# K read by quarters of 512 rows of 16 items and turned contiguously, softmax over two batch rows, five V buffers, and wo behind V: a decode layer on one core

## The chip, the core and the metric

The kernel runs on one core of one Trainium2 chip. What counts is the device time of one execution in microseconds (us). The core's engines work side by side and each takes its own instructions in order: TensorE (PE) multiplies matrices, VectorE (DVE), ScalarE (ACT) and GpSimd (POOL) work on vectors, and SyncE (SP) issues transfers (DMA) on one queue. An instruction or a transfer can wait for others by semaphores, and then all that stands behind it on its engine or queue waits too.

## What is computed

One token for each of 8 batch rows goes through attention and an MLP, each behind a layer norm. There are 32 query heads of width 128 and 8 K/V heads, so 4 query heads share one. Of 8192 cached rows the last 2048 count. The reference, cut:

```
B, D, F = 8, 512, 1792
Hq, Hkv, Sk, Dh, W = 32, 8, 8192, 128, 2048
q = layernorm(x) @ wq                            # wq is 512 x 4096
scores = einsum("bhqd,bhkd->bhqk", q, k_cache[:, :, Sk - W:]) * Dh ** -0.5
p = softmax(scores)
o = einsum("bhqk,bhkd->bhqd", p, v_cache[:, :, Sk - W:])
h = x + o @ wo                                   # wo is 4096 x 512
u = layernorm(h)
out = h + u + gelu(layernorm(u) @ w3) @ w4       # w3 is 512 x 1792, w4 is 1792 x 512
```

The branch of w1 and w2 shifts tokens, and with one token it is zero. All data are bf16. The K and V rows that count are 33.5 MB each, wq and wo 4.2 MB each, w3 and w4 1.8 MB each. An item below is one batch row with one K/V head: 64 items of 2048 rows.

## The kernel before

The work on K goes in 16 tiles of 2 MB. Tile n is batch row n // 2 and 4 of its 8 heads, with all 2048 rows, in two buffers (`knat`). `load` (L627) puts 64 consecutive rows, 16 KB, on each partition; the partition is 4 times the row block (32 of them) plus the head.

`turn_K` (L327) turns a tile on VectorE by transposes of 32x32 blocks of f32, each f32 being two bf16, into `kT_sb`, in four instructions of 128x1024. Its write pattern is scattered: the four heads, which lie side by side in a block, go to places 2 KB apart, so that each head's 512 columns stand in one run for PE:

```
src = knat[:, n % NK, :].bitcast(dt.float32).rearrange("p (c h x) -> p h c x", h=2, x=32)
dst = kT_sb[:, n % NK, :].bitcast(dt.float32).rearrange("p (h t n) -> p h t n", h=2, t=KQ)
parts = [(src[:, h, lo:hi], dst[:, h, :, 8 * lo:8 * hi].rearrange("p t (c a) -> p c a t", a=8))]
```

For the last batch row the pieces are 128x512, eight to a tile.

`pe_QK` (L341) multiplies a tile with a block-diagonal arrangement of q (`qblk`, copied by `keep_q`, L299, half on ScalarE and half on VectorE) into a bank of PSUM for the batch row (`S_ps`). After two tiles a batch row has its scores as 128x512, and the softmax runs: `row_max`, `head_max` (L356 to L368, VectorE), `row_exp` (L370, ScalarE), `turn_P` (L390, a VectorE transpose of 128x512 bf16), `move_P` (L402, 16 small matmuls), `spread_P` (L415, four ScalarE copies into `pT_sb`), and for the sums `row_sums` and `head_sums` (L377 to L387).

V comes in tiles of the same form in three buffers (`vnat`). `pe_PV` (L438) multiplies one with the spread P in 16 matmuls of 512 columns into `o_rows`; `o_parts` (L450) splits the result into two bf16 parts, one copied by ScalarE (L451), the other subtracted by VectorE (L452); `pe_oT` (L455) selects the right columns with matmuls (L461), and `scale` (L468) divides by the sums into `oT_all`. The last V tile comes in four loads of 512 KB with runs of 1 KB and goes another way (`turn_last`, `pe_PVi`).

The order on each engine is written out in `plan` (L528 to L564): each step gets a slot, and the steps are issued by rising slot. For tile n the four transposes have n, n + 0.1, n + 0.2 and n + 0.3, `pe_QK` n + 0.48, `pe_PV` of tile n - 2 comes at n + 0.55, its `o_parts` at n + 1.07 and `pe_oT` at n + 1.22. So on VectorE the subtraction for PV n - 2 stands between the first and the second transpose of tile n + 1, and on PE PV n - 2 stands behind QK n.

The transfers are one list on SP's queue (L642 to L658): wq, K0, K1, then K and V in turns, the first half of wo, the last whole V, the second half of wo, four quarters of the last V, w3 and w4. K n waits for the transposes of tile n - 2, V n for PV n - 3; wo goes into the place of wq (`wbig`), in runs of 1 KB.

The end: `pe_wo_row` (L494) multiplies 16 heads with wo into rows, split and added by `pe_h0` (L509); `pe_wo` (L518) adds the other heads; then come the layer norm (L575 on), `pe_w3` (L590), gelu, w4 (L660 on) and the store.

Of the kernel before, what the change touches and what calls it, by code (L numbers as in the profile page):

```python
# [6 lines left out]
dt = mybir.dt  # L7
ACT = mybir.ActivationFunctionType
ALU = mybir.AluOpType
# [19 lines left out]
NV = 3  # L29
NQ = B * G // KQ  # L30
CQ = W // 32
NR = 4
FQ = CQ * DH

# [31 lines left out]
def bass_sequential_preLN__sliding_block_cached__mixer_s_mlp__decode_kernel(  # L66
# [23 lines left out]
    with es:  # L90
# [8 lines left out]
        sel_f = sb([128, H], dt.float32, "sel_f")  # L99
# [4 lines left out]
        wo_v = wbig[:, :].rearrange("p (h n) -> p h n", h=H)  # L104
        knat = sb([128, NK, FQ], dt.bfloat16, "knat")
        vnat = sb([128, NV, FQ], dt.bfloat16, "vnat")


        kT_sb = sb([128, NK, FQ], dt.bfloat16, "kT_sb")

        w3_sb = knat[:, 1, 0:KC * F].rearrange("p (k f) -> p k f", k=KC)
        w4_sb = kT_sb[:, 0, 0:FC * D].rearrange("p (k n) -> p k n", k=FC)
# [20 lines left out]
        qblk = sb([128, 2, 4 * KQ * B, H], dt.bfloat16, "qblk")  # L133

        P_sb = sb([128, 2, 512], dt.bfloat16, "P_sb")
        pB_sb = sb([128, 2, 512], dt.bfloat16, "pB_sb")

        pT_sb = sb([128, 2, 2, CQ, KQ * R], dt.bfloat16, "pT_sb")
        pL_sb = sb([128, KQ, KQ, KQ * R], dt.bfloat16, "pL_sb")
        mx = sb([128, 32], dt.float32, "mx")  # L140
        mxT = sb([128, 32], dt.float32, "mxT")
        nm = sb([128, 2 * R], dt.float32, "nm")
        neg = sb([128, 2, 32], dt.float32, "neg")
        lcol = sb([128, 2], dt.float32, "lcol")
        lsel = sb([128, H], dt.float32, "lsel")
        rL = sb([128, 2, H], dt.float32, "rL")

        oT_all = sb([128, H, 32], dt.bfloat16, "oT_all")
# [6 lines left out]
        orow = sb([128, 2, 512], dt.bfloat16, "orow")  # L155
# [17 lines left out]
        kb_ps = ps_t([128, 4 * 512], dt.float32, "kb_ps")  # L173
        kbank = [kb_ps[:, 512 * i:512 * (i + 1)] for i in range(4)]
        S_ps = [ps_t([128, 512], dt.float32, f"S_ps{i}") for i in range(2)]
        sm = ps_t([128, 512], dt.float32, "sm")
        pT_ps = sm[:, 0:256].bitcast(dt.bfloat16)
        LB = slice(416, 448)
        o_rows = ps_t([128, 512], dt.float32, "o_rows")
# [3 lines left out]
        sem_vi = [S(f"sem_vi{i}") for i in range(KQ)]  # L183
        sem_wo = [S(f"sem_wo{i}") for i in range(2)]
# [28 lines left out]
        e_qz = clear(qblk[:, :, :, :].rearrange("p j n h -> p (j n h)").bitcast(dt.float32))  # L213
# [8 lines left out]
        e_oz = PO.op(lambda e: e.memset(oT_all[:], 0.0))  # L222
# [4 lines left out]
        e_sel = DV.op(lambda e: e.tensor_reduce(sel_f[:, :].rearrange("p (y r) -> p y r", r=R),  # L227
# [45 lines left out]

        e_qblk = [[], []]
        e_qd = []
        for j in range(2):
            qT_ps = (o_rows[:, 0:256].bitcast(dt.bfloat16), pT_ps)[j]
# [436 lines left out]
```

## Time and profile before

| | |
|---|---|
| median of 3 runs | 234.0 us (232.34 to 234.56) |
| the profiled execution's own time | 233.2 us |
| its span, from the first to the last instruction | 231.4 us |
| mean granted clock of TensorE | 0.652 of full speed |
| busy: PE, VectorE, ScalarE | 104.8, 156.2, 48.0 us |
| read from HBM | 79.18 MB |

The profile comes from one execution. Its slices cut the span into 40 equal parts; a digit is the busy share of an engine in tenths. In the timeline a line is start, duration, engine, the line of the kernel, the operation, what it writes and reads with partitions x elements, how many instructions are drawn together, and in brackets how long the engine had been idle and what ended that. In the groups by form, the columns behind the count are the busy time in us, the mean duration of one in ns, and the idle time before. In the answers by window the columns are the window, its length, the busy time of PE, PE's weight loads, VectorE, ScalarE and GpSimd (each with its count), the granted clock, the DMA share and GB/s. Matmuls overlap, so a single one's duration says less than the distance between groups.

### The profile page before, as it was taken

How to read it: one execution, taken by the hardware profiler on the slowest of the kernel's cores; microseconds unless marked ns; L12 is line 12 of the kernel's file. 1: busy time of each engine (PE TensorE's matmuls, PEld its weight loads, DVE VectorE, ACT ScalarE, POOL GpSimd, SP SyncE). 2: the span in 40 equal slices, each digit the busy share in tenths (PEclk: the TensorE clock that was granted, in tenths of full speed). 3: DMA queues.
4: the chain of work that ended last, by engine and by line, in shares of the span. 5: the costliest groups of instructions: out<-in, count | busy, mean ns of one | idle time of the engine just before them, and what ended most of it. 6: DMA issues, size and time to landing. Idle time of an engine off the chain costs nothing.

```text
span 231.4 us, 2574 instructions
## 1 busy us (share of the span) xinstructions
PE 104.8 (45%) x1086; PEld 44.4 (19%) x1086; DVE 156.2 (68%) x200; ACT 48.0 (21%) x80; POOL 4.6 (2%) x17
## 2 busy tenths in 40 slices
PE   0061303270917082717352654446353726287593
PEld 0020000120212021202121221112021302023383
DVE  4219996939694969586976698569946994742222
ACT  7414001410140015011501060106010511022402
POOL 4000000000000000000000000000000000000002
PEclk9996555566576657575757575757575667567755
DMA  7997499999896989697969796989698999999900
GB/s 273 453 402 323 181 411 388 416 340 409 317 411 255 388 357 416 241 442 303 425 241 425 297 413 270 411 334 428 241 394 334 397 398 423 383 386 410 366 12 1
DMA packets 13291, 79.34 MB, mean 343 GB/s; under 512 B 728, under 2 KB 8672, under 8 KB 9184
## 3 DMA queue, kind: packets, MB, share of 16 engines
q1 hardware_dynamic: 13264, 79.18, 85.5%
q8 instruction: 8, 0.13, 0.2%
q14 instruction: 3, 0.02, 0.0%
q10 hardware_dynamic: 16, 0.01, 0.0%
HBM read 79.18 MB, written 0.01 MB: 342 GB/s over the span
## 4 chain that ended last, share of the span: by engine, by line
DVE 44%; PE 37%; DMA 7%; ACT 5%; issue 5%; SPq 0%; ACTq 0%; DVEq 0%
DVE kT_sb L338 35%; PE o_rows L444 21%; PE S_ps L348 12%; DMA knat<-in_A_k_cache_dram 7%; DVE orow L452 4%; ACT orow L451 4%; DVE qblk L306 1%; PE S_ps L522 1%; PE S_ps L666 1%; DVE pB_sb L396 1%; ACT pT_sb L419 1%; ACT L619 1%; PE kb_ps L481 1%; DVE oT_all L469 1%; DVE rL L385 0%
## 5 line engine op out<-in xcount | busy, mean ns | idle before, releaser
L338 DVE STREAM_TRANSPOSE kT_sb<-knat 128x1024 f32<-128x1024 f32 (+1 forms) x72 | 118.4, 1725 | 0.7 <-DMA knat<-in_A_k_cache_dram 0.7
L348 PE MATMUL S_ps<-kT_sb,qblk 128*32 128x512 bf16 x256 | 30.4, 623 | 85.6 <-DVE kT_sb L338 85.6
L444 PE MATMUL o_rows<-vnat,pT_sb 128*64 128x512 bf16 x240 | 48.2, 574 | 1.0 <-ACT pT_sb L419 1.0
L452 DVE TENSOR_TENSOR orow<-o_rows,orow 128x512 bf16<-128x512 f32 x15 | 10.4, 691 | 30.6 <-ACT orow L451 30.6
L348 PEld LDWEIGHTS S_ps<-kT_sb,qblk 128*32 128x32 bf16 x256 | 7.1, 126 | 96.7 <-DVE kT_sb L338 88.0
L444 PEld LDWEIGHTS o_rows<-vnat,pT_sb 128*64 128x64 bf16 x240 | 17.7, 157 | 32.9 <-issue 31.5
L451 ACT ACTIVATE orow<-o_rows 128x512 bf16<-128x512 f32 x15 | 9.0, 597 | 70.7 <-PE o_rows L444 70.7
L373 ACT ACTIVATE P_sb<-S_ps,neg 128x512 bf16<-128x512 f32 x8 | 5.5, 687 | 84.9 <-DVE neg L368 84.9
L419 ACT ACTIVATE pT_sb<-kb_ps,mask 128x512 bf16<-128x512 f32 (+1 forms) x32 | 18.5, 661 | 4.9 <-PE kb_ps L410 4.9
L357 DVE TENSOR_REDUCE mx<-S_ps 128x1 f32<-128x512 f32 x8 | 5.5, 692 | 16.0 <-PE S_ps L348 16.0
L461 PE MATMUL o_rows<-sel,orow 128*128 128x16 bf16 x120 | 5.4, 171 | 13.4 <-DVE orow L452 13.4
L461 PEld LDWEIGHTS o_rows<-sel,orow 128*128 128x128 bf16 x120 | 4.0, 96 | 18.3 <-DVE orow L452 18.3
L410 PE MATMUL kb_ps<-pB_sb,perm 128*32 128x128 bf16 (+1 forms) x128 | 3.4, 227 | 7.3 <-DVE pB_sb L396 7.3
L271 DVE TENSOR_SCALAR qrow<-S_ps 128x512 bf16<-128x512 f32 x1 | 0.7, 691 | 8.9 <-PE S_ps L263 8.9
L263 PE MATMUL S_ps<-wbig,xlnT 128*32 128x512 bf16 x32 | 3.3, 584 | 7.3 <-DMA wbig<-in_A_wq_dram 7.3
L396 DVE STREAM_TRANSPOSE pB_sb<-P_sb 128x512 bf16<-128x512 bf16 x8 | 5.8, 724 | 0.0
L620 POOL TENSOR_SCALAR r<-vsum 128x8 f32<-128x8 f32 x1 | 0.2, 243 | 219.9 <-DVE vsum L604 219.9
L410 PEld LDWEIGHTS kb_ps<-pB_sb,perm 128*32 128x32 bf16 x128 | 1.9, 98 | 13.8 <-DVE pB_sb L396 13.8
L212 ACT ACTIVATE qblk<-zero 128x4096 f32<-128x4096 f32 x1 | 3.6, 3599 | 0.0
L383 PE MATMUL sm<-lsel,ones_f 128*128 128x32 f32 x16 | 3.5, 302 | 0.0
L469 DVE TENSOR_TENSOR oT_all<-o_rows,rL 128x16 bf16<-128x16 f32 x15 | 3.0, 198 | 0.6 <-PE o_rows L461 0.5
L263 PEld LDWEIGHTS S_ps<-wbig,xlnT 128*32 128x32 bf16 x32 | 1.2, 138 | 8.9 <-issue 8.9
(96 smaller groups left out, 66.1 us busy)
## 6 DMA issues: line engine op xcount, KB each, us to landing
knat<-in_A_k_cache_dram SPq DMA_DIRECT2D x16, 2048.0 KB, 9.2
vnat<-in_A_v_cache_dram SPq DMA_DIRECT2D x15, 2048.0 KB, 14.0
wbig<-in_A_wq_dram SPq DMA_DIRECT2D x1, 4096.0 KB, 12.2
wbig<-in_A_wo_dram SPq DMA_DIRECT2D x2, 2048.0 KB, 16.9
vnat<-in_A_v_cache_dram SPq DMA_DIRECT2D x4, 512.0 KB, 7.9
knat<-in_B_w_dram SPq DMA_DIRECT2D x1, 1792.0 KB, 10.9
kT_sb<-in_B_w_dram SPq DMA_DIRECT2D x1, 896.0 KB, 12.0
kT_sb<-in_B_w_dram SPq DMA_DIRECT2D x1, 768.0 KB, 12.7
```

The lines of the kernel that those rows point to most:

```text
L338: e_KT[n] = DV.op(lambda e, s=s, d=d: e.transpose(d, s), K(n), e_QK.get(n - NK))
L348: ins = e.matmul(S_ps[b % 2][32 * t:32 * (t + 1), :], qblk[:, j, (hp * KQ + t) * B + b, :], kv[:, hp // 2, hp % 2, t], start=(j == 0 and h ...
L357: e_max[b] = DV.op(lambda e: e.tensor_reduce(mx[:, 0:1], S_ps[b % 2][:, :], AX.X, ALU.max), e_QK[2 * b + 1], e_mx, e_mT.get(b - 1))
L373: e_exp[b] = AC.op(lambda e: e.activation(dst, src, ACT.Exp, bias=neg[:, j, 0:1], scale=1.0, accum_out=lcol[:, j:j + 1]), e_negc[b], e_pB. ...
L396: e_pB[b] = DV.op(lambda e: e.transpose(dst, src), e_exp[b], e_perm.get(b - 2))
L410: ins = e.matmul(dst[:, c], perm[:, c, :], src, start=True, stop=True, tile_position=(0, 32 * g), skip_group_check=True)
L419: e_expand[b] = AC.op(lambda e, t=t, dst=dst: e.activation(dst, pP[:, 0:256 * nj].rearrange("p (n r) -> p n r", r=R), ACT.Copy, scale=mask ...
L444: ins = e.matmul(o_rows[64 * u:64 * (u + 1), :], pT_sb[:, b % 2, j, 4 * c:4 * (c + 1), :], vbuf(q)[:, 512 * c:512 * (c + 1)], start=(c < 2 ...
L451: e = AC.op(lambda e: e.activation(orow[:, 0, :], o_rows[:, :], ACT.Copy), e_PV[q], before[0])
L452: e_olo[q] = DV.op(lambda e: e.tensor_tensor(orow[:, 1, :], o_rows[:, :], orow[:, 0, :], ALU.subtract), e)
L461: ins = e.matmul(o_rows[:, 0:KQ * R], orow[:, part, c * DH:(c + 1) * DH], sel64[:, KQ * R * c:KQ * R * (c + 1)], start=(c == 0 and part == 0),
L469: return DV.op(lambda e: e.tensor_tensor(oT_all[:, heads, b], src, rL[:, b % 2, heads], ALU.mult), e_rL[b], e_oz, *waits)
```

## The change

A K tile is now a quarter of the rows (512) of all 16 items of two batch rows, again 2 MB with 64 rows of 16 KB on each partition; the partition is 8 times the item plus the row block (8 of them). `turn_K` reads and writes contiguously, 128x1024 f32 four times a tile for every tile. `pe_QK` therefore reads its columns in runs of 8 elements. Scores of two batch rows stand in two banks (`S_all`) after four tiles, and the softmax is done for both at once: one maximum and one exp over 1024 elements, one transpose of P of 128x1024, 16 matmuls and eight spreads. q is copied into `qblk` by ScalarE alone.

V has five buffers, three in `vnat` and two in the place of wq, and a load waits for the PV five tiles back, or, for the first five, for the matmuls of q. PV of tile v stands at slot v + 4.55, with two banks for its result; the last four V tiles are multiplied in pieces of 256 columns (`NARROW`), 32 matmuls in four column groups. The special way of the last V tile is gone.

wo comes behind the last V, in the place of K (`knat`), in three pieces with runs of 4 KB, and waits for the last transposes of K; `turn_o` rearranges the attention output for that order. w3 and w4 go into the two buffers of `kT_sb`. The diff, cut to its core:

```diff
-NV = 3
+NV = 5
...
+NP = B // 2
...
-        vnat = sb([128, NV, FQ], dt.bfloat16, "vnat")
+        vnat = sb([128, 3, FQ], dt.bfloat16, "vnat")
+        vbuf = [vnat[:, i, :] for i in range(3)] + [wbig[:, i * FQ:(i + 1) * FQ] for i in range(2)]
...
-        w3_sb = knat[:, 1, 0:KC * F].rearrange("p (k f) -> p k f", k=KC)
-        w4_sb = kT_sb[:, 0, 0:FC * D].rearrange("p (k n) -> p k n", k=FC)
+        wo_v = knat[:, :, :].rearrange("p i (m k n) -> p (i m) k n", k=4, n=D)
+        w3_sb = kT_sb[:, 0, 0:KC * F].rearrange("p (k f) -> p k f", k=KC)
+        w4_sb = kT_sb[:, 1, 0:FC * D].rearrange("p (k n) -> p k n", k=FC)
...
+        e_qblk = None
+        for f in range(4):
+            j = f % 2
+            src = kbank[j][32 * f:32 * (f + 1), :].rearrange("p (y i x r) -> p x y i r", y=16, x=2, r=R)[:, f // 2]
+            dst = qblk[32 * f:32 * (f + 1), :, 16 + R * f:16 + R * (f + 1)].rearrange("p (y i) r -> p y i r", i=NP)
+            e_qblk = AC.op(lambda e, dst=dst, src=src: e.activation(dst, src, ACT.Copy), e_qd[j], e_qz)
...
        def turn_K(n, i):
-            src = knat[:, n % NK, :].bitcast(dt.float32).rearrange("p (c h x) -> p h c x", h=2, x=32)
-            dst = kT_sb[:, n % NK, :].bitcast(dt.float32).rearrange("p (h t n) -> p h t n", h=2, t=KQ)
-            h, k = divmod(i, 2)
-            if n // 2 < LAST:
-                lo, hi = CQ // 2 * k, CQ // 2 * (k + 1)
-                parts = [(src[:, h, lo:hi], dst[:, h, :, 8 * lo:8 * hi].rearrange("p t (c a) -> p c a t", a=8))]
-            else:
-                parts = [(src[:, h].rearrange("p (c m) x -> p m c x", m=4)[:, m],
-                          dst[:, h].rearrange("p t (m a c) -> p m c a t", m=4, a=8)[:, m]) for m in (2 * k, 2 * k + 1)]
-            for s, d in parts:
-                e_KT[n] = DV.op(lambda e, s=s, d=d: e.transpose(d, s), K(n), e_QK.get(n - NK))
+            w = FQ // 2 // 4
+            src, dst = (x[:, n % NK, :].bitcast(dt.float32)[:, w * i:w * (i + 1)] for x in (knat, kT_sb))
+            e_KT[n] = DV.op(lambda e: e.transpose(dst, src), K(n), e_QK.get(n - NK))
...
-            kv = kT_sb[:, n % NK, :].rearrange("p (h t n y) -> p h y t n", h=2, t=KQ, y=2)
+            p, g = divmod(n, 4)
+            kv = kT_sb[:, n % NK, :].rearrange("p (c h t a y) -> p h y t c a", c=CQ, h=2, t=KQ, a=8)
+            w = 16 - 16 * (g % 2)
...
+            e_QK[n] = PE.op(f, e_KT[n], e_qblk, e_exp.get(p - 1))
+        def row_max(p):
+            e_max[p] = DV.op(lambda e: e.tensor_reduce(mx[:, 0:1], S_all[:, :], AX.X, ALU.max),
+                             e_QK[4 * p + 3], e_mx, e_mT.get(p - 1))
...
+        def row_exp(p):
+            i = p % 2
+            e_exp[p] = AC.op(lambda e: e.activation(P_sb[:, :], S_all[:, :], ACT.Exp, bias=neg[:, i, 0:1],
+                                                    scale=1.0, accum_out=lcol[:, i:i + 1]),
+                             e_negc[p], e_pB.get(p - 1), e_lsel.get(p - 2))
...
+        def turn_P(p):
+            e_pB[p] = DV.op(lambda e: e.transpose(pB_sb[:, :], P_sb[:, :]), e_exp[p], e_perm.get(p - 1))
...
+            e_perm[p] = PE.op(f, e_pB[p], e_perm0, e_spread.get(p - 1), e_qblk)
+        def spread_P(p):
+            pv = pT_sb[:, p % 2, :, :, :].rearrange("p f (k c) x -> p (f k) c x", c=KQ)
+            for i in range(2):
+                for t in range(KQ):
+                    e_spread[p] = AC.op(lambda e, t=t, i=i: e.activation(
+                        pv[:, :, 2 * i:2 * i + 2, R * t:R * (t + 1)],
+                        kbank[i].rearrange("p (y c r) -> p y c r", c=2, r=R), ACT.Copy, scale=mask4[:, t:t + 1]),
+                        e_perm[p], e_pz, e_mask, e_PV.get(4 * p - 5))
...
+        def width(v):
+            return 2 if v in NARROW else 4
+        def pe_PV(v):
+            w = width(v)
+            n, m = 8 // w, KQ * R * w
+            def f(e):
+                for c in range(CQ // w):
+                    u = c % n
+                    ins = e.matmul(o_rows[v % 2][m * u:m * (u + 1), 0:w * DH],
+                                   pT_sb[:, v // 4 % 2, v % 4, w * c:w * (c + 1), :],
+                                   vbuf[v % NV][:, w * DH * c:w * DH * (c + 1)], start=(c < n), stop=(c >= CQ // w - n),
+                                   tile_position=(0, m * u), skip_group_check=True)
+                return ins
+            e_PV[v] = PE.op(f, V(v), e_spread[v // 4], e_sc.get(v - 2))
...
+        def o_parts(v):
+            cs = slice(0, width(v) * DH)
+            e = AC.op(lambda e: e.activation(orow[:, v % 2, 0, cs], o_rows[v % 2][:, cs], ACT.Copy), e_PV[v], e_oT.get(v - 2))
+            e_olo[v] = DV.op(lambda e: e.tensor_tensor(orow[:, v % 2, 1, cs], o_rows[v % 2][:, cs], orow[:, v % 2, 0, cs],
+                                                       ALU.subtract), e)
...
+            e_oT[v] = PE.op(f, e_olo[v], e_selb)
+            b, j = divmod(v, 2)
+            e_sc[v] = DV.op(lambda e: e.tensor_tensor(oT_all[:, KQ * R * j:KQ * R * (j + 1), b], dst,
+                                                      rL[:, v // 4 % 2, v % 4, :], ALU.mult), e_rL[v // 4], e_oT[v])
+        def turn_o():
+            dst = kbank[0][:, 0:4 * G * B]
+            def f(e):
+                for k in range(4):
+                    for r in range(R):
+                        ins = e.matmul(dst[32 * r:32 * (r + 1), G * B * k:G * B * (k + 1)],
+                                       ident_b[:, :].rearrange("p (x k) -> p k x", k=4)[:, k],
+                                       oT_all[:, :, :].rearrange("p (m r) b -> p r m b", r=R)[:, r],
+                                       start=True, stop=True, tile_position=(0, 32 * r), skip_group_check=True)
+                return ins
+            e = PE.op(f, e_sc[NQ - 1], e_spread[NP - 1])
+            return DV.op(lambda e: e.tensor_copy(ow_sb[:, :, :, 0:B].rearrange("p m k b -> p k m b"),
+                                                 dst.rearrange("p (k m b) -> p k m b", k=4, m=G)), e, e_oz)
...
+        def pe_wo_row(lo, hi, *waits):
+            def f(e):
+                for m in range(lo, hi):
+                    for k in range(4):
+                        ins = e.matmul(hrow[32 * k:32 * (k + 1), :], ow_sb[:, m, k, :], wo_v[:, m, k, :],
+                                       start=(m == 0), stop=(m == NB_ROW - 1 and k > 0),
+                                       tile_position=(0, 32 * k), skip_group_check=True)
+                if hi == NB_ROW:
+                    ins = e.matmul(hrow[0:32, :], ident_b[0:B, 0:32], x_sb[:, :], start=False, stop=True,
+                                   tile_position=(0, 0), skip_group_check=True)
+                return ins
+            return PE.op(f, *waits)
+        def pe_wo():
+            def f(e):
+                for m in range(NB_ROW, G):
+                    for k in range(4):
+                        for nb in range(KC):
+                            ins = e.matmul(hT_ps[:, nb * B:(nb + 1) * B], wo_v[:, m, k, nb * 128:(nb + 1) * 128],
+                                           ow_sb[:, m, k, 0:B], start=(m == NB_ROW and k == 0 and nb == 0), stop=False,
+                                           skip_group_check=True)
+                return ins
+            PE.op(f, (sem_wo[2], 16), e_exp[NP - 1])
...
+        NARROW = range(12, 16)
...
+        for p in range(NP):
+            n = 4 * p + 3
+            late = 1 if p < NP - 1 else 0.7
+            at(n + 0.62, row_max, p)
+            at(n + 0.64, head_max, p)
+            at(n + 0.66, row_exp, p)
+            at(n + late + 0.05, turn_P, p)
+            at(n + late + 0.06, row_sums, p)
+            at(n + late + 0.15, move_P, p)
+            at(n + late + 0.16, spread_P, p)
+            at(n + late + 0.20, head_sums, p)
+        for v in range(NQ - 4):
+            at(v + 4.55, pe_PV, v)
+            at(v + 5.07, o_parts, v)
+            at(v + 5.22, pe_oT, v)
+        for slot, fn, v in ((16.50, pe_PV, 12), (16.55, o_parts, 12), (16.60, pe_PV, 13), (16.62, pe_oT, 12),
+                            (16.65, o_parts, 13), (17.05, pe_PV, 14), (17.06, pe_oT, 13), (17.10, o_parts, 14),
+                            (17.30, pe_oT, 14), (17.55, pe_PV, 15), (17.65, o_parts, 15), (17.75, pe_oT, 15)):
+            at(slot, fn, v)
...
+        e_ow = turn_o()
+        pe_wo_row(0, 4, e_ow, (sem_wo[0], 16), e_spread[NP - 1])
+        e_rows = pe_wo_row(4, NB_ROW, (sem_wo[1], 16), X, e_idb)
+        pe_wo()
+        pe_h0(e_rows)
...
-        def load(q, src, dst, sem, *waits):
-            b, g = q // 2, q % 2 * KQ
-            dma(SP, dst, src[b, g:g + KQ, W0:SK, :].rearrange("t (a c) d -> a t (c d)", c=CQ), sem, *waits)
         def load_k(n):
-            load(n, A_k_cache, knat[:, n % NK, :], K(n)[0], e_KT.get(n - NK))
-        def load_v(q):
-            load(q, A_v_cache, vbuf(q), V(q)[0], e_PV.get(q - NV))
-        def load_wo(n):
-            hh = H // 2
-            dma(SP, wo_v[:, n * hh:(n + 1) * hh, :],
-                A_wo[n * hh * DH:(n + 1) * hh * DH, :].rearrange("(h p) n -> p h n", p=DH), sem_wo[n], e_q)
-        load_k(0)
-        load_k(1)
-        for n in range(2, NQ):
+            p, g = divmod(n, 4)
+            lo = W0 + W // 4 * g
+            dma(SP, knat[:, n % NK, :],
+                A_k_cache[2 * p:2 * p + 2, :, lo:lo + W // 4, :].rearrange("b g (a c) d -> (b g) a (c d)", c=CQ),
+                K(n)[0], e_KT.get(n - NK))
+        def load_v(v):
+            b, g = v // 2, v % 2 * KQ
+            dma(SP, vbuf[v % NV], A_v_cache[b, g:g + KQ, W0:SK, :].rearrange("t (a c) d -> a t (c d)", c=CQ),
+                V(v)[0], e_PV.get(v - NV, e_q))
+        nv = 0
+        for n in range(NQ):
             load_k(n)
-            load_v(n - 2)
-        load_wo(0)
-        load_v(NQ - 2)
-        load_wo(1)
-        for t in range(KQ):
-            dma(SP, vnat[:, 0, NC * DH * t:NC * DH * (t + 1)].rearrange("p (g x) -> p g x", g=4),
-                A_v_cache[LAST, KQ + t, W0:SK, :].rearrange("(g x m) d -> x g (m d)", g=4, m=4), sem_vi[t], e_PV[NQ - 4])
-        dma(SP, w3_sb, B_w3.rearrange("(k p) f -> p k f", p=128), sem_w3, e_KT[NQ - 1])
+            if n in (1, 3) or 5 <= n < NQ - 2 or n == NQ - 1:
+                load_v(nv)
+                nv += 1
+        for v in range(nv, NQ):
+            load_v(v)
+        wo_src = A_wo.rearrange("(m p k) n -> p m k n", p=128, k=4)
+        for n, (lo, hi) in enumerate(((0, 4), (4, NB_ROW), (NB_ROW, G))):
+            dma(SP, wo_v[:, lo:hi, :, :], wo_src[:, lo:hi, :, :], sem_wo[n], e_KT[NQ - 1])
-        dma(SP, w3_sb, B_w3.rearrange("(k p) f -> p k f", p=128), sem_w3, e_KT[NQ - 1])
+        dma(SP, w3_sb, B_w3.rearrange("(k p) f -> p k f", p=128), sem_w3, e_QK[NQ - 2])
...
-            dma(SP, w4_sb[:, lo:hi, :], w4_src[:, lo:hi, :], sem_w4[n], e_QK[NQ - 2])
+            dma(SP, w4_sb[:, lo:hi, :], w4_src[:, lo:hi, :], sem_w4[n], e_QK[NQ - 1])
```

## The prediction

> **What bounds the kernel now.** I read the page's slices and chain first, then the chain of waits in order of time, the timeline of one round, the groups by form and the transfer rate by windows.
>
> ```profile
> span 231.4 us, 2574 instructions
> ...
> PE   0061303270917082717352654446353726287593
> ...
> DVE  4219996939694969586976698569946994742222
> ...
> DMA  7997499999896989697969796989698999999900
> ...
> DVE 44%; PE 37%; DMA 7%; ACT 5%; issue 5%; SPq 0%; ACTq 0%; DVEq 0%
> ```
>
> PE and VectorE (DVE) take turns: where one is busy the other is not. They share 81% of the chain, while the transfers stand at 6 to 9 tenths. One round, one 2 MB K tile (n = 3), in the timeline:
>
> ```profile
> 46.38 1.90 PE L348 MATMUL S_ps<-kT_sb,qblk 128*32 128x512 bf16 x16 [4.53 <-DVE kT_sb L338]
> ...
> 48.20 2.78 PE L444 MATMUL o_rows<-vnat,pT_sb 128*64 128x512 bf16 x16
> 51.03 0.60 ACT L451 ACTIVATE orow<-o_rows 128x512 bf16<-128x512 f32 x1 [7.27 <-PE o_rows L444]
> 51.66 0.69 DVE L452 TENSOR_TENSOR orow<-o_rows,orow 128x512 bf16<-128x512 f32 x1 [3.48 <-ACT orow L451]
> 52.27 3.68 DVE L338 STREAM_TRANSPOSE kT_sb<-knat 128x1024 f32<-128x1024 f32 x2
> ...
> 55.80 0.22 DVE L469 TENSOR_TENSOR oT_all<-o_rows,rL 128x16 bf16<-128x16 f32 x1
> 55.83 1.93 DVE L338 STREAM_TRANSPOSE kT_sb<-knat 128x1024 f32<-128x1024 f32 x1
> ...
> 57.81 1.90 PE L348 MATMUL S_ps<-kT_sb,qblk 128*32 128x512 bf16 x16 [5.05 <-DVE kT_sb L338]
> ```
>
> It is a ring: scores (QK), then PV, which stands behind QK on PE, then ScalarE's copy, then VectorE's subtraction, behind which three of the next tile's four transposes are queued, then the next QK. 1.82 + 2.83 + 0.63 + 0.61 + 5.54 = 11.43 us from QK to QK. In the other phase PV takes 3.67 to its copy, at the lower granted clock (QK at 57.81, PV 59.64, copy 63.31, next QK 70.31). From the fifth QK (70.31) to the sixteenth (201.12) a round is 11.89 us on average.
>
> ```profile
> L338 DVE STREAM_TRANSPOSE kT_sb<-knat 128x1024 f32<-128x1024 f32 x56 | 103.6, 1925 | 0.7 <-DMA knat<-in_A_k_cache_dram 0.7
> L338 DVE STREAM_TRANSPOSE kT_sb<-knat 128x512 f32<-128x512 f32 x16 | 14.7, 1028 | 0.0
> ...
> L396 DVE STREAM_TRANSPOSE pB_sb<-P_sb 128x512 bf16<-128x512 bf16 x8 | 5.8, 724 | 0.0
> ```
>
> ```profile
> 13.00:19.00 6.00, 4.63 (x48) 2.14 (x48) 1.93 (x2) 2.17 (x5) 0.00 (x0) 1.00 1.00 429
> 20.00:22.00 2.00, 0.00 (x0) 0.00 (x0) 2.00 (x2) 0.57 (x1) 0.00 (x0) 0.50 0.86 369
> 22.00:24.00 2.00, 0.00 (x0) 0.00 (x0) 2.00 (x2) 0.00 (x0) 0.00 (x0) 0.50 0.00 0
> 28.00:42.00 14.00, 3.08 (x34) 1.30 (x34) 11.89 (x12) 1.44 (x4) 0.00 (x0) 0.50 1.00 410
> 124.00:136.00 12.00, 6.48 (x58) 2.50 (x58) 9.63 (x13) 1.58 (x4) 0.00 (x0) 0.57 0.91 366
> ```
>
> The last two columns are the DMA share and GB/s. Full, the queue moves 410 to 429 GB/s: I take 420, 5.0 us for 2 MB, so 10.0 us for one K and one V. A round of 11.89 leaves slack. At 22 to 26 us nothing moves: the third K waits for the first tile's transposes, and the first V is queued behind it.
>
> **The change, part by part.**
>
> *Contiguous transposes.* No row shows a contiguous f32 transpose. Nearest is L396: 512 bf16 elements, seven times 660 to 681 ns, and 1090 ns the one time its source is permuted. Scattered f32 costs the same as scattered bf16 (1028 and 1090 for 512), so I take the types as equal when contiguous too: from 212 ns (128x32, L362) to 670 (512) is 0.95 ns an element, 1.16 us for 1024; back to back the present ones are 1.80 apart at 1.925 each, 0.12 less, so 1.04. Ends: 1.04 and 1.80 (no gain). I take 1.10. Three stand in the ring: 2.1 us a round. The fourth hides behind QK and PV as now. Without that cover it would cost 1.1.
>
> *QK* now reads runs of 8 elements with jumps of 256 B. Nearest is move_P (L410), which reads runs of 4 with jumps and takes 232 ns for 128 columns against 222 for L293's contiguous ones: nothing to 5%, and I take nothing. The upper end is the scattered DVE ratio, 1090/670 = 1.63: 1.2 us a round.
>
> *A plain round:* 1.83 + 3.25 (mean of 2.83 and 3.67) + 0.63 + 0.61 + 3 x 1.10 + 0.14 (scale) + 0.08 = 9.84 us.
>
> *Softmax per two rows* comes every fourth round. VectorE's maximum over 1024 from 692 plus about 0.53, exp likewise from 0.69 to about 1.11 plus 0.19, and P's transpose 1.1 instead of 0.6 delay the subtraction: from QK, maximum and negation end at 3.83, K's first transpose at 4.93, exp at 5.25, P's transpose at 6.37, sums at 6.49, subtraction done at 7.10 (6.73 now). Plus 3.52 and 0.25 for the reciprocal: 10.87. The eight spreads on ScalarE (four take 2.42 now, so 4.84) end before the next QK does. q's block copies leave VectorE (2.8 us at 24.8) for ScalarE, idle there. The clears on ScalarE and the POOL memset change size under the load of wq, which lands at 13.0; if that cover went, 1 to 2 us of them would show.
>
> *The queue.* K0 and K1 are through at 21.7 as now; V0 waits only for q's matmuls (done 16.3) and fills the gap. At 5.0 each: V0 26.7, K2 31.7, K3 36.7, V1 41.7, K4 46.7. K0 was through at about 16.9 by bytes and its transpose began at 17.8, so K4 is usable at 47.7. Five 1.10, sums and reciprocal: fifth QK at 53.7, against 70.3. PV lags four tiles, not two, so no PV stands in the first four rounds. After that a pair takes 10.0 and the ring 9.84 or 10.87: nearly equal, queue at most 3 us ahead. Five V buffers each come free two rounds before reuse, so they cost nothing; a V that came late would stop all K queued behind it on SP. One new wait bites: K14 and K15 have no V between them, and K15 waits for tile 13's transposes, so the queue idles some 4 us near 142. V11 to V15, wo and the MLP weights stand behind it.
>
> *Sixteenth QK:* 53.7 + 9 x 9.84 + 2 x 10.87 = 164.0, against 201.1.
>
> *The tail* is longer. From that QK: exp done 5.3, P's transpose 6.4, move_P 7.0, eight spreads 11.9, then ScalarE's copy of PV 11, queued behind them, 12.6, subtraction 13.2, its selection 13.7. Only then four narrow PVs; each is half of L444's columns (about 1.8) plus half-width copy, subtraction, selection, partly overlapped: 10.0 to 23.7. turn_o and its copy 0.8: 24.5. wo: 25 matmuls from L498's 16 in 1.05, 2.3; copy and subtraction 1.4 with the rest of wo beside; pe_h0 0.45; from hsum to the end 8.87 (222.63 to 231.4, and a gap). Sum 37.5, against 30.3 now. wo lands before it is wanted: K15 through 149.5, five V 174.5, wo 184.5, w3 189, w4 193.5 (385 GB/s in 1 KB runs): about 198 by that road. wo's longer runs thus save nothing on the path; if the tail were 4 us shorter they would. The wo wait moves from q's matmul to the last K transposes, met at 163.
>
> Span 164.0 + 37.5 = 201.5. The profiled execution took 233.2 with span 231.4, 1.8 outside, so 203.3. It lies 0.8 under the median of 234.0; I say 203.
>
> **Rivals.**
>
> *K's pieces collide (slower side).* Now a load's 128 pieces of 16 KB lie at 32 offsets in each of 4 heads; after, at 8 offsets in each of 16 items, which are 2 MB apart (8192 x 128 x 2 bytes) and are read side by side at equal offsets. If each K load takes d longer, a pair takes 10 + d, and 16 loads delay all by 16 d: d = 0.5 gives 211, d = 1.9 (6.9 us, 304 GB/s) gives 234, and from there it is slower; at d = 3 it is 251. Slowest saturated row now: 380 GB/s at 186 to 194 us, in part 1 KB runs, 5.5 us. For it: every load now has another pattern. Against: nothing yet shows a rate that low. [...]
>
> *The transposes stay at 1.80.* Then the ring loses 11 x 2.1 = 23 again and the fifth tile's start some 2: 203 + 25 = 228. For it: no contiguous f32 row. Against: 670 to 1090 within L396.
>
> *QK's jumps cost 1.2 a round:* 11 to 14 rounds, about 218. Against: L410.
>
> *Transfers bind:* at 400 GB/s a pair is 10.5; 11 x 0.4 and seven loads x 0.24 at the start, less 3 of slack: about 206. This lies in the forecast's own range.
>
> **How the numbers follow.** Forecast 0.62 (198 to 210); K's pieces mildly slow 0.16 (210 to 230); transposes unchanged 0.06; QK slow 0.06; K's pieces at d over 1.9, slower, 0.10. About 1% is what a measurement of this kernel can tell from no change. Faster 0.88 (all but the last, less 0.02 that lies near 234), same 0.02, slower 0.10. Low end 196: transposes at 1.04 and every PV at 2.83 take 11 x (0.18 + 0.42) = 6.6 off. High end 222 leaves out about 2 in 10.
>
> **What would show it.** L338's successor near 1.1 apart; QK to QK near 9.9; the fifth QK near 54, the sixteenth near 164; transfers at 9 tenths from 3 us to 190 with one dip near 142; 37 us after the last QK. If K's rate falls under 380 GB/s where only K moves, or QK exceeds 1.9 us, the forecast is wrong there.

## The result, and the profile after

The changed kernel takes 305.3 us (303.2 to 319.3, four runs) against 233.6 (232.3 to 234.6, four runs): 1.305 times as long, with an interval of 1.294 to 1.315. The forecast was 203, with 196 to 222. The execution first profiled was a disturbed one (319.3 us), so the lines here are of a second run of the same kernel: 307.0 us, span 305.2.

> The changed kernel once more, unaltered, for a profile of an undisturbed execution: about 304 us, K alone near 210 GB/s.

The page of the changed kernel, its slices and its chain:

```profile
span 305.2 us, 2364 instructions
...
PE   0232011120445060050451406052273306445545
...
DVE  5006606441770420621706033170726043732212
...
DMA  8999999999999999999699997989778999999940
GB/s 336 320 223 208 346 213 210 324 243 208 256 288 246 286 202 296 230 303 228 232 221 307 219 271 189 210 281 213 265 178 174 217 303 380 432 412 420 344 149 16
...
DMA 75%; DVE 16%; PE 5%; ACT 2%; issue 1%; SPq 0%; DVEq 0%
DMA knat<-in_A_k_cache_dram 69%; DVE kT_sb L322 12%; DMA kT_sb<-in_B_w_dram 6%; PE o_rows L410 2%; ACT pT_sb L393 2%; DVE orow L420 1%; PE S_all L333 1%; DVE pB_sb L373 1%; DVE mx L342 0%; ACT P_sb L356 0%; SPq L194 0%; ACT orow L419 0%; DV
```

PE and VectorE took turns before; now both mostly wait, and K's loads alone are 69% of the chain (transfers: 7% before). The DMA digits are at 9 almost throughout and look like a queue at its limit, but the line under them says what this busy queue moves: in the first eight slices 208 to 223 GB/s where K is loaded and 320 to 346 where the slice holds wq or a V; at the end, where only V, wo and the MLP weights are left, 380 to 432. Here a busy share says that the transfer engines have work, not how many bytes flow.

The timeline of tiles 1 to 3:

```profile
32.99 4.62 DVE L322 STREAM_TRANSPOSE kT_sb<-knat 128x1024 f32<-128x1024 f32 x4 [5.21 <-DMA knat<-in_A_k_cache_dram]
37.67 1.90 PE L333 MATMUL S_all<-kT_sb,qblk 128*32 128x512 bf16 x16 [7.93 <-DVE kT_sb L322]
...
47.92 4.62 DVE L322 STREAM_TRANSPOSE kT_sb<-knat 128x1024 f32<-128x1024 f32 x4 [10.30 <-DMA knat<-in_A_k_cache_dram]
...
57.68 4.63 DVE L322 STREAM_TRANSPOSE kT_sb<-knat 128x1024 f32<-128x1024 f32 x4 [5.14 <-DMA knat<-in_A_k_cache_dram]
62.36 1.90 PE L333 MATMUL S_all<-kT_sb,qblk 128*32 128x512 bf16 x16 [7.87 <-DVE kT_sb L322]
```

K2 and K3 follow each other in the queue, and their first transposes are 9.76 us apart (47.92, 57.68). In between VectorE turns one tile in 4.6 and waits 5.1. The transposes in the groups by form (busy us, mean ns, idle before):

```profile
L322 DVE STREAM_TRANSPOSE kT_sb<-knat 128x1024 f32<-128x1024 f32 x64 | 76.2, 1222 | 147.8 <-DMA knat<-in_A_k_cache_dram 147.8
```

The transposes are as contiguous and as quick as forecast, and QK takes its 1.90 us. The 147.8 us of waiting for K are new (0.7 before). By windows (the last two columns are the DMA share and GB/s), with K0 and K1 in the first, V0 in the second, K2 and K3 in the third:

```profile
13.40:33.00 19.60, 6.67 (x64) 2.60 (x64) 5.32 (x6) 2.83 (x7) 0.00 (x0) 0.67 0.99 217
33.10:38.10 5.00, 0.43 (x8) 0.16 (x12) 4.51 (x4) 0.00 (x0) 0.00 (x0) 0.50 1.08 400
38.20:57.70 19.50, 3.27 (x32) 0.64 (x24) 4.64 (x5) 0.00 (x0) 0.00 (x0) 0.50 0.99 218
```

Same queue, same 2 MB, same 128 pieces of 16 KB: a K load takes 9.8 us, a V load 5.0 to 5.2. In the trace a piece of K takes 1.22 us, one of V 0.61, with all 16 transfer engines at work on both (shares 0.99 and 1.08). From 60 us on it gets worse. The trace has 16 landings for each load, one for each part of it, and one or more of them now come later than the rest: the last one 3.3 us behind the middle one for the K load that lands at 75.5, 15.3 for the one at 144.0. V's loads no longer take 5 us beside K's, and some pairs of K and V take 20 us instead of 14.8.

### The profile page after: what moved, and what is told of

It reads as the page before. It is cut to its first block, busy times and chain, and to the rows that moved or that the text cites. A ratio compares the mean times of both kernels' runs of the same rounds, so it can differ in the third digit from the quotient of the medians.

```text
span 317.5 us, 2364 instructions
## 1 busy us (share of the span) xinstructions
PE 101.2 (32%) x1010; PEld 42.7 (13%) x1010; DVE 108.0 (34%) x158; ACT 45.2 (14%) x73; POOL 4.6 (1%) x17
## 4 chain that ended last, share of the span: by engine, by line
DMA 75%; DVE 17%; PE 4%; ACT 2%; SPq 1%; issue 1%
DMA knat<-in_A_k_cache_dram 69%; DVE kT_sb L322 12%; DMA kT_sb<-in_B_w_dram 5%; PE o_rows L410 2%; ACT pT_sb L393 1%; DVE pB_sb L373 1%; DVE orow L420 1%; PE S_all L333 1%; SPq L194 1%; DVE rL L367 0%; DVE mx L342 0%; ACT P_sb L356 0%; ACT orow L419 0%; PE S_all L635 0%; PE kb_ps L384 0%
## 5 line engine op out<-in xcount | busy, mean ns | idle before, releaser
L322 DVE STREAM_TRANSPOSE kT_sb<-knat 128x1024 f32<-128x1024 f32 x64 | 76.2, 1221 | 159.8 <-DMA knat<-in_A_k_cache_dram 159.8
L333 PE MATMUL S_all<-kT_sb,qblk 128*32 128x512 bf16 x256 | 30.4, 623 | 72.8 <-DVE kT_sb L322 72.8
L410 PE MATMUL o_rows<-vnat,pT_sb 128*64 128x512 bf16 (+1 forms) x192 | 29.2, 505 | 0.1
L419 ACT ACTIVATE orow<-o_rows 128x512 bf16<-128x512 f32 (+1 forms) x16 | 8.7, 546 | 118.5 <-PE o_rows L410 118.5
L393 ACT ACTIVATE pT_sb<-kb_ps,mask 128x512 bf16<-128x512 f32 x32 | 18.9, 702 | 36.6 <-PE kb_ps L384 36.6
L333 PEld LDWEIGHTS S_all<-kT_sb,qblk 128*32 128x32 bf16 x256 | 7.1, 126 | 85.6 <-DVE kT_sb L322 76.9
L410 PE MATMUL o_rows<-wbig,pT_sb 128*64 128x512 bf16 (+1 forms) x128 | 16.6, 493 | 0.5 <-DVE oT_all L438 0.5
L410 PEld LDWEIGHTS o_rows<-vnat,pT_sb 128*64 128x64 bf16 (+1 forms) x192 | 11.7, 148 | 18.6 <-issue 18.0
L420 DVE TENSOR_TENSOR orow<-o_rows,orow 128x512 bf16<-128x512 f32 (+1 forms) x16 | 9.7, 607 | 8.9 <-ACT orow L419 8.8
L410 PEld LDWEIGHTS o_rows<-wbig,pT_sb 128*64 128x64 bf16 (+1 forms) x128 | 7.2, 152 | 10.0 <-issue 8.9
```

Source lines behind the costliest of these rows:

```text
L322: e_KT[n] = DV.op(lambda e: e.transpose(dst, src), K(n), e_QK.get(n - NK))
L333: ins = e.matmul(S_ps[g // 2][32 * t:32 * (t + 1), :], qblk[:, (hp * KQ + t) * NP + p, w:w + 32], kv[:, hp // 2, hp % 2, t], start=(g % 2 ...
L393: e_spread[p] = AC.op(lambda e, t=t, i=i: e.activation(pv[:, :, 2 * i:2 * i + 2, R * t:R * (t + 1)], kbank[i].rearrange("p (y c r) -> p y ...
L410: ins = e.matmul(o_rows[v % 2][m * u:m * (u + 1), 0:w * DH], pT_sb[:, v // 4 % 2, v % 4, w * c:w * (c + 1), :], vbuf[v % NV][:, w * DH * c ...
L419: e = AC.op(lambda e: e.activation(orow[:, v % 2, 0, cs], o_rows[v % 2][:, cs], ACT.Copy), e_PV[v], e_oT.get(v - 2))
L420: e_olo[v] = DV.op(lambda e: e.tensor_tensor(orow[:, v % 2, 1, cs], o_rows[v % 2][:, cs], orow[:, v % 2, 0, cs], ALU.subtract), e)
```

## The experiments

Theory A was that of the prediction's rival: K's 16 streams lie 2 MB apart and collide in HBM. Theory B: the shape of the load, 16 groups of 8 partitions, is slow whatever its addresses.

**K in the old shape.** Of the changed kernel, only the source of the K load:

```diff
-                A_k_cache[2 * p:2 * p + 2, :, lo:lo + W // 4, :].rearrange("b g (a c) d -> (b g) a (c d)", c=CQ),
+                A_k_cache[n // 2, n % 2 * KQ:n % 2 * KQ + KQ, W0:SK, :].rearrange("t (a c) d -> a t (c d)", c=CQ),
```

> The changed kernel with one thing undone: K is loaded in the pattern of before (4 heads, all rows), so the scores are of other rows; everything else, waits and order too, stays. Under A and B alike K loads take about 5 us again. If the load pattern is all that was wrong with the prediction: 203 us, QK to QK 9.8, fifth QK near 54, 37 us after the last QK. A rival: V is slow by itself in the changed order (five buffers, two in the place of wq), or the longer tail costs more; then it stays above 220.

204.2 us (203.2 to 205.3), 0.876 of before (0.871 to 0.881); the span is 202.1. Its DMA and GB/s slices, and two windows with K alone:

```profile
DMA  7989999999999999999999999999389999999990
GB/s 274 441 379 444 425 428 441 428 425 435 431 363 439 315 431 425 425 425 435 399 412 328 441 412 428 431 436 402 143 334 425 431 435 428 428 388 413 413 348 20
```

```profile
13.00:22.00 9.00, 5.16 (x48) 2.29 (x48) 4.88 (x5) 2.83 (x7) 0.00 (x0) 0.94 1.01 431
33.00:42.00 9.00, 1.96 (x20) 0.52 (x24) 8.64 (x8) 0.00 (x0) 0.00 (x0) 0.50 1.01 430
```

All of the loss is in that one line: where K is loaded the DMA share is that of the changed kernel, the rate double.

**Loads alone, and other addresses.** A kernel of loads only, eight stretches of four loads of 2 MB: (1) 32 blocks by 4 heads, (2) 16 items by 8 at 2 MB, (3) the same at 2 MB and 16 KB, (4) at 144 KB, (5) 32 by 4 at 80 KB, (6) 32 by 4 at 2 MB, (7) one run, (8) as (2). And the changed kernel with its items 2 MB and 16 KB apart.

> Nothing but loads: eight stretches, each of four 2 MB loads into the same four buffers, each stretch waiting for the one before; the rest of the layer is left out. In order: (1) the pattern of before, 4 heads x 32 row blocks; (2) the pattern after, 16 items x 8 blocks, items 2 MB apart; (3) the same with items 2 MB + 16 KB apart; (4) the same with items 144 KB apart; (5) 32 pieces of 64 KB, 80 KB apart; (6) 32 pieces of 64 KB, 2 MB apart; (7) 2 MB in one run; (8) as (2). Theory A, addresses in HBM: items a multiple of 2 MB apart and read at equal offsets share what can deliver only half, so (2), (6) and (8) run near 210 GB/s and (3), (4), (5) near 420. Theory B, the shape: 16 groups of 8 partitions go to the engines so that only half of the ways into the core's memory work at a time, so (2), (3), (4) and (8) run near 210 whatever the addresses, and (5), (6) as their own shape makes them. Both: (1) and (7) near 420.

> The changed kernel with K items 2 MB + 16 KB apart in place of 2 MB, so the scores are of other rows; shape, destination and order of the load are those of the changed kernel. Theory A: K loads at about 5 us, 203 to 210 us in all. Theory B: nothing changes, about 304 us, K alone near 210 GB/s.

Stretches 1 to 6 of the loads alone (window, length, GpSimd, clock, DMA share, GB/s; each begins with some 3 us before the first bytes are in):

```profile
0.70:22.90 22.20, 0.19 (x1) 1.00 0.90 378
22.90:65.00 42.10, 0.00 (x0) 1.00 0.92 199
65.10:106.20 41.10, 0.00 (x0) 1.00 0.94 204
106.30:148.70 42.40, 0.00 (x0) 1.00 0.93 198
148.80:171.70 22.90, 0.00 (x0) 1.00 0.88 366
171.80:194.70 22.90, 0.00 (x0) 1.00 0.89 366
```

From landing to landing that is 4.9 us a load for every 32 by 4, at a pitch of 80 KB as at 2 MB, and 9.6 to 9.8 for nearly every 16 by 8, at 144 KB as at 2 MB. One run of 2 MB, the seventh stretch, also takes 4.9. The changed kernel with 16 KB more between items took 304.1 us (297.5 to 309.4), where theory A asked for 203 to 210: its quickest executions lie 2% under the changed kernel's, and its first K loads still land 9.4 to 9.6 us apart. Theory A is false, theory B holds.

**The pattern in the kernel before.** Only the same source of K put into the kernel before.

> The kernel before with one thing done: K is loaded in the changed pattern (16 items, a quarter of the rows), so the scores are mixed up; all else stays. If the pattern alone is slow, whatever the kernel, a K load takes about 9.8 us and a pair of K and V 14.7 in place of the ring's 11.9: 234 + 16 x 2.8, about 280 us. If the slowness needs the changed kernel around it, about 234.

321.8 us in one execution, span 320.1. The direction is right, and the size is not: 280 took a K load at 9.8 and a V load at 5, but V's loads slowed too, and pairs took 16 to 22 us.

**More shapes.** Stretches of 64 groups by 2 partitions, 8 by 16 and 4 by 32, and then 24 loads in which 16 by 8 and 32 by 4 take turns.

> Nothing but loads again. Three stretches of four 2 MB loads by other shapes, all at pitches that are no power of two: 64 groups of 2 partitions, 8 groups of 16, 4 groups of 32; then 24 loads with four in flight, by turns the changed K pattern (16 x 8) and V's (32 x 4), which no engine's work disturbs. If half the engines were left out, the DMA share would be near 0.5 with pieces as quick as ever; if all share a way that is too narrow, the share stays near 1 with pieces twice as long (16 x 8 showed 0.92 to 1.1). I expect 8 x 16 at 210 GB/s and 4 x 32 at 105 with few engines, 64 x 2 at 420 if small groups are the good ones. By turns: 9.7 + 4.9 = 14.6 us a pair (287 GB/s) if a V load is as quick as ever behind a slow K; 20 us (210 GB/s), as in the changed kernel after 90 us, if mixing the two patterns itself slows V, without any work of PE or VectorE beside it.

The three stretches in order, and the loads by turns:

```profile
0.70:22.90 22.20, 0.20 (x1) 1.00 0.91 378
23.60:99.00 75.40, 0.00 (x0) 1.00 0.49 111
99.60:196.00 96.40, 0.00 (x0) 1.00 0.24 87
198.00:380.00 182.00, 0.00 (x0) 1.00 1.00 277
```

64 by 2 is fast (4.9 us a load). 8 by 16 leaves the share at 0.49, half of the transfer engines, and each of those is slow as well (about 1.2 us a piece, not 0.61): 111 GB/s, not the 210 expected, which had halved the engines and not the pieces. 4 by 32 leaves a quarter (0.24): 87 GB/s; its pieces began at 1.1 us and took 0.61 in the last two loads, 19.5 us each. So in these three stretches the share follows the outer dimension: 0.91 at 64, 0.49 at 8, 0.24 at 4. That 16 groups give each engine eight neighbouring partitions is a guess from this, which the next run puts to use; no trace names the partitions of an engine. By turns, a pair takes 15.1 us (9.9 and 5.2), all through the 24 loads: mixing the two shapes by itself hardly slows V.

**Why 16 by 8 is slow.** Theory B1: the engines walk through their eight partitions in step, and what they write at one time shares ways into SBUF by twos. B2: the shape is slow by itself.

> Only transfers; all of the layer's computation is left out. Five stretches, each of four loads: (1) 16 groups of 8 partitions, as the changed kernel loads K, 2 MB each; (2) 32 groups of 2 on partitions 0 to 63, 1 MB each; (3) four heads by 32 blocks, 2 MB; (4) as (1), but behind one load as in (3) and two small ones that occupy first the engines 0 to 3, then 0 to 11, so that each engine runs four pieces of 16 KB apart from the one four numbers away; (5) as (1). Theory B1: pieces are dealt to the 16 transfer engines by the outer dimension, eight neighbouring partitions to an engine when it is 16; the engines walk through their eight in step, and what they write at one time goes through half of the ways into SBUF, two engines to each. [...] Under B1 stretch 4 runs at the full rate, 4.9 us from landing to landing, pieces of 0.61 us, though its loads are those of stretch 1, which keep 9.7; and stretch 2, on 64 partitions, takes 4.9 us for 1 MB, though cut into 32 groups. Theory B2: 16 groups of 8 is slow by itself (descriptors, or the order of reading HBM): stretch 4 keeps 9.7 us and 1.2 us a piece, and stretch 2 runs at 2.45 us for 1 MB. Stretch 3 4.9 and stretch 5 9.7 under both, since a stretch that begins with idle engines has them in step.

```profile
0.70:42.80 42.10, 0.19 (x1) 1.00 0.93 199
42.90:66.00 23.10, 0.00 (x0) 1.00 0.87 182
66.10:88.20 22.10, 0.00 (x0) 1.00 0.91 380
105.30:125.80 20.50, 0.00 (x0) 1.00 0.85 344
125.90:168.30 42.40, 0.00 (x0) 1.00 0.93 198
```

The fourth line decides it: the same loads as in the first and the fifth, behind two small ones meant to put the engines four pieces apart, land 5.0 to 5.2 us from each other, not 9.7, with pieces of 0.65 us. And the second line: 32 groups on 64 partitions take 5.0 to 5.1 us for each 1 MB. The times are those of B1 in both, and B2 is out. What the fourth line shows is that the loads ahead of them decide between 5.0 to 5.2 us and 9.7. That the engines share ways into SBUF by twos is B1's assumption; no run shows such ways, and none stood behind B1's 4.9 us for 64 partitions. What stays open is how 32 groups of 4 are dealt: they take 4.9 us, and no run shows the dealing.

**Can the kernel be freed of it?** First with those two small loads between wq and K0, then with GpSimd as the issuer of all loads behind wq, in the same order:

```diff
+        for lo, m in ((0, 4), (16, 12)):
+            dma(SP, ahead[lo:lo + 4 * m, :],
+                rows[0:512 * m, :].rearrange("(i s) d -> i s d", s=512)[:, 0:4 * CQ, :].rearrange("i (a c) d -> i a (c d)", c=CQ),
+                sem_a)
```

> The changed kernel whole, with two small loads of K rows that nobody uses between wq and K0: 64 KB on each of the engines 0 to 3, then 64 KB on each of 0 to 11, as in the fourth stretch of the run loads3. Nothing else is changed. There they put engines that share a way into SBUF four pieces apart, and the same loads came every 5.2 us instead of every 9.7. Theory B1 (engines in step share ways): as long as the queue never runs dry the engines keep their distance. At first it does not run dry: K0 lands 5 us later on the slowest engines (22.8), and K loads take 5.2 us: QK starts near 27.5, 32.5, 42, 47. In the rounds after that a K load is issued only 2 to 4 us before the load ahead of it lands (in the version with K by four heads: issued 64.3, the V ahead of it landed from 66.4 to 68.2), so the engines that are 5 us ahead fall idle and lose part of the distance. If they keep 2.4 us, the whole takes 204 + 5 = 209 us; if they fall back into step from the first such round on, the remaining eleven K loads take 9.7 and the whole comes to 209 + 11 x 4.7 = 261; so 209 to 261, and K's pieces of 0.61 us in the first 50 us in any case. The rival, that a start in step is not what makes these loads slow in the kernel, where V's loads stand between them: 305 plus the 5 us of the added loads, 310, and pieces of 1.2 us from K0 on.

> The changed kernel whole, with K, V, wo, w3 and w4 issued by GpSimd in the same order, not by SyncE; wq stays on SyncE. Sources, places in SBUF and all other instructions stay. What it tells: whether the loads of K are slow because of how the issuing queue deals the pieces to the 16 transfer engines (eight neighbouring partitions to an engine where the outer dimension is 16), or whatever deals them. [...] If GpSimd deals by partitions, K's pieces of 16 KB take 0.61 us and a load 4.9 as in the version with K by four heads (204.2 us), plus for each of 16 K loads and 16 V loads whatever GpSimd takes longer to issue; no run shows that yet; with up to 1 us that is not hidden on 11 pairs, 204 to 215 us. If GpSimd deals by the outer dimension as well, pieces of 1.2 us, K loads of 9.7 and 300 to 320 us as now.

The first took 309.5 us (303.1 to 316.0) and lies outside B1's own 209 to 261. From 20 to 30 us, as K0 lands, a piece did take 0.68 us (median), little over half of what the rival said, but from 30 us on most are at 1.1 to 1.2 again: K1's parts land 7.2 us behind K0's, and V0's 9.5 behind those. So the step that failed in this expectation was that V's loads do no harm. That some engines then write V while others write K, and that these collide as well, would explain it; no run shows it. GpSimd's queue took 307.8 us, 1.310 of before (1.295 to 1.324), and its K loads land 9.7 to 9.9 us apart: the loads are as slow from either queue, and how either deals the pieces to the engines no trace shows.

The landings of the changed kernel, ever more spread from 60 us on, look like those of the first of the two, and the trace shows what comes ahead of the spread. The changed kernel's page lists eight transfers of 16 KB on another queue, of the kind that it calls instruction:

```profile
q8 instruction: 8, 0.13, 0.2%
```

From K0 on, the 16 parts of each load land within 0.9 us of each other. The first of these eight transfers starts at 58.2 us, and in the load then under way, V1, one part lands 2.9 us after all the others. The distance from first to last part then grows from V load to V load (3.8, 6.6, 12.4, 16.1, 19.3 us), and the K loads between leave it as it is. In the three other kernels with this K load from their start, the first late part also comes in the load during the first such transfer (58.5 us in the one with 16 KB more between items, 58.6 with GpSimd's queue, 52.8 in the kernel before with K by items). The loads by turns have no such transfer, and their parts stay within 1.2 us to the end. With K by four heads one part falls back too, at 41.5 us, but the distance stays under 4.2 us. No run takes these transfers away, so that they start the drift, and that the pairs of 20 us come from it, is argued and not tested by itself.

**What the rest of the change is worth in the old layout.** The kernel before with contiguous transposes for seven batch rows and QK's columns taken accordingly; then the same with V n - 2 ahead of K n in the queue; then everything of the change but K by items (PV two tiles behind K, softmax per batch row):

```diff
-                parts = [(src[:, h, lo:hi], dst[:, h, :, 8 * lo:8 * hi].rearrange("p t (c a) -> p c a t", a=8))]
+                w = FQ // 2 // 4
+                parts = [tuple(x[:, n % NK, :].bitcast(dt.float32)[:, w * i:w * (i + 1)] for x in (knat, kT_sb))]
...
-            kv = kT_sb[:, n % NK, :].rearrange("p (h t n y) -> p h y t n", h=2, t=KQ, y=2)
+                kv = kT_sb[:, n % NK, :].rearrange("p (c h a t y) -> p h y t c a", c=CQ, h=2, a=8, t=KQ)
```

> The kernel before with the contiguous transposes alone, for the first seven batch rows; loads, order and softmax stay, the output is the reference's. QK then reads single elements of 4 bytes 16 bytes apart. If the transposes were the bound and QK reads that at full rate: a round of 9.9 to 10.2 instead of 11.9 for some 13 rounds, 23 less: 208 to 212 us. If QK pays for the jumps (1.2 us a round): about 222. If contiguous transposes are worth nothing without the rest: 233.

> As before_contig, and each V load is issued ahead of the K load that it stood behind, so that the first V fills the gap at 22 to 26 us. If the queue bounds the rounds by then, 3 to 5 us less than before_contig; if the ring bounds them, no difference.

> A version that computes the layer whole: the changed kernel's contiguous transposes, five V buffers, wo behind V in 4 KB runs and its narrow last products, but with K by four heads and 32 blocks as before, the softmax per batch row as before, and PV two tiles behind K, not four; K and V take turns on the queue from V0 on. If the loads of K by items were all that was wrong with the change, this is paced by the queue: K0 and K1 are through at 21.7, K4 at 51.7, so the fifth QK comes near 57.5, a pair of K and V takes 10.0, K15 is through near 162 and the sixteenth QK comes near 167.5. V15 is through at 172, wo at 182, w3 and w4 at 191. From the sixteenth QK: softmax and spreads 8, two narrow PVs 6, the rearranging of the output 1, wo 4, the rest 9: 28, so span 196, 198 us; 196 to 205 with the drops of the granted clock. The version with only the transposes contiguous took 218, and the changed kernel with K by four heads, whose scores are those of other rows, 204. The rival, that the softmax per batch row with PV close behind it sits in the ring and makes rounds of 11 us instead of 10, gives 11 us more: 209.

218.3 us (217.0 to 218.5; 0.935 of before, 0.930 to 0.939), 219.3 (0.938, 0.930 to 0.946) and 218.3 (0.935, 0.929 to 0.941). All three beat both kernels, and none reaches what was expected of the best case. V ahead of K makes no difference, so by that expectation the ring and not the queue paces the rounds. One round of the first:

```profile
86.09 3.88 PE L351 MATMUL S_ps<-kT_sb,qblk 128*32 128x512 bf16 x16 [3.35 <-DVE kT_sb L338]
...
89.90 2.12 PE L447 MATMUL o_rows<-vnat,pT_sb 128*64 128x512 bf16 x16
...
93.30 2.36 DVE L338 STREAM_TRANSPOSE kT_sb<-knat 128x1024 f32<-128x1024 f32 x2
```

Two transposes take 2.36, as forecast, but QK takes 3.85 instead of 1.90. With four heads side by side in a block, one head's columns are 16 bytes apart when nothing scatters them; by items they are 4 bytes apart in runs of 8. So the gain of three transposes (1.9 us) moves to PE as 1.95 us in the same ring. What the ring still gains (11.0 us a round, not 11.9, from the fifth QK to the fourteenth) comes with a shorter PV, 1.9 to 2.3 us in most rounds, not 2.7 to 3.6, at a mean granted clock of 0.78, not 0.65; why the clock is higher no run shows. The expectation of the third version had left out these 3.85, though the first version's trace showed them: QK to QK is 11.1 us, its fifth QK at 63.4, its sixteenth at 185.6. Why steps of 16 bytes take QK 3.85 us and steps of 4 bytes 1.90, no run shows.

That is also the limit of the first experiment's 204 us: its QK reads in the order of the items and takes 1.90, so its scores are not those of the layer. K by items is what makes contiguous transposes free on PE, and the load by items is what gives it back. One way out was not tried: tiles of 256 rows of 32 items. The loads alone have that load as their sixth stretch, 32 by 4 at 2 MB, and it takes 4.9 us. An item's columns would then stand 4 bytes apart in runs of 4, and the softmax would wait for eight tiles; what QK takes there no run shows.

## Why the prediction was wrong, point by point

**The step that failed** is the one on the queue: "At 5.0 each: V0 26.7, K2 31.7". A K load takes 9.8. The time was counted in bytes at 420 GB/s, and a rate measured with loads of 32 groups by 4 was carried to one of 16 by 8. The prediction's own sign of this, K's rate under 380 GB/s where only K moves, came: 217. The sum of what followed: the fifth QK at 81.9 instead of 53.7 (28.2 us), eleven rounds of 16.6 instead of 10.0 (72.1), and 40.9 behind the sixteenth QK instead of 37.5 (3.4): 103.7, which with 201.5 is the span of 305.2. Of the first 28.2, five K loads at 4.8 make 24, and the late part of the fifth (3.3) most of the rest. Of the eleven rounds' 72.1, 4.8 a K load make 53; the other 19 are in the pairs in which V's loads slow too.

**The slower rival** named the place and gave its price as 16 d with the bend at d = 1.9. d was 4.8: by that formula 203 + 77 = 280, and the remaining 25 us are the late parts and what V's loads lost with them, which the formula had at zero. Its mechanism was wrong, addresses 2 MB apart: at 144 KB the load is as slow (9.6 to 9.8 us), and 32 by 4 at 2 MB takes 4.9. What was not weighed is how the engines come to a load: the same 16 by 8 takes 9.7 us, or 5.0 to 5.2 behind two small loads. The chance of 0.10 had little to stand on: "every load now has another pattern" was all that the profile could say, and no row bounded from above what a new pattern costs.

**The transposes** were right: 4.62 us for four, 1.16 apart where 1.10 was taken. The rival that 1.80 would stay was wrong.

**QK's jumps** cost nothing as taken: 1.90. The upper end, 1.2 us a round, was passed in the old layout, where the step is 16 bytes: 1.95 us a round.

**The ring, the softmax and the tail** held, as the version with K in the old shape shows: fifth QK 54.65 (53.7), rounds of 9.7 to 10.1 (9.84) and 11.1 with the softmax (10.87), sixteenth QK 166.2 (164.0), 35.9 behind it (37.5), 204.2 in all (203).

**The queue's dip** near 142, for K15 behind tile 13, came in the version with K in the old shape: 143 GB/s in the slice from 141.5 to 146.5.

**Transfers bind** held in a way not meant: the queue bound the kernel, at half its rate.

## What to carry to other kernels

A load's time is not its bytes over a rate: its shape decides too (here 2 MB took 4.9 us in 32 or 64 groups and 9.6 to 9.8 in 16, at busy shares of 0.88 to 0.94), so time a new shape alone before a layout is built on it. Look at GB/s beside the busy share; a share of 9 tenths at half the rate (here 0.99 at 217 GB/s, against 1.01 at 431) is a queue in trouble, not a queue well used. A layout that suits one engine can be paid for where the others read it (here QK took 3.85 us, not 1.90): count the load's shape, the transpose's stride and the matmul's step together.

## What the runs showed of the hardware

- 2 MB into 128 partitions in pieces of 16 KB: 4.9 us with 32 groups of 4 or 64 of 2, 9.6 to 9.8 with 16 of 8, at any pitch tried; with 8 groups of 16 the busy share is 0.49, with 4 of 32 it is 0.24.
- The same 16-by-8 loads take 5.0 to 5.2 us behind two small loads meant to put the engines four pieces apart, with nothing else loaded. In the kernel, with V's loads beside K's, most pieces were back at 1.1 to 1.2 us from 30 us on.
- The parts of a load began to land apart with the first 16 KB transfer of the kind instruction, and with loads of two shapes in the queue the distance grew to some 20 us; with one shape it stayed under 4.2, and without such transfers it stayed within 1.2.
- QK over 512 columns and 16 matmuls: 1.90 us with columns 4 bytes apart in runs of 8, 3.85 with columns 16 bytes apart.
- A contiguous f32 transpose of 128x1024 takes 1.22 us, 1.16 to 1.18 from one to the next; scattered it took 1.93, 1.80 from one to the next.
